# Loading V as rows of eight tokens and building its key spans on the chip

## The chip, the cores and the metric

The kernel runs on one core of one Trainium2 chip. The metric is the time of one execution in device microseconds. The program has the whole problem in one launch.

## The reference, cut to what matters

```python
q, k, v: (8, 8, 576, 64) float32            # batch, heads, tokens, head size
w_in: (512, 2048), w_out: (2048, 512)
scores = (q @ k.T) / 8, masked to 0 <= i - j < 64
attn   = softmax(scores) @ v
x      = attn as (8*576, 8*64)
h      = x @ w_in
out    = (h - tanh(h)) @ w_out               # (4608, 512)
```

A query sees itself and the 63 tokens before it. So a block of 64 queries needs 128 keys: its own block and the one before.

## The kernel before, in words

The work is in two kinds. **Attention** goes by pairs of heads: pair g is heads pr and pr + 4 of batch b, with g = 4b + pr, so there are 32 pairs. For each pair `load_qk` (L68) loads q and k on 72 partitions, each with 8 consecutive tokens of both heads (2 KB runs), on SP's queue. `cast` (L75) makes bf16 rows, mostly on GpSimd (POOL). `tr` (L150) transposes the rows on PE, 8 transposes each for q and for k, and moves the result out of PSUM: q's first head by ACT and its second by DVE, k by ACT. `scores` (L164) makes three groups of three 128x128 score tiles, keys on partitions, and ACT takes the exponential. `masking` (L172) multiplies by a mask on DVE. `pv` (L176) multiplies the three probability tiles of a group with V; a column of ones beside V gives the sums, DVE takes their reciprocal and scales the two heads. `x_tr` (L190) transposes the attention output of two pairs into the columns that the next stage reads. Tokens inside a block of 64 stand in a permuted order, which the mask and the output stores undo.

**V** stands in `vw`: for each block of 64 queries the lower 64 partitions hold the keys of the block before, the upper 64 those of the block itself, with 129 columns (two heads and the ones). `load_v` (L89) fills the upper half straight from HBM on POOL's software queue, which casts on the way, in runs of 64 numbers (256 bytes). `shift_v` (L95) copies the upper half to the lower half, one block further on, by an SBUF-to-SBUF DMA on SP.

**The two matrix products** go by chunks of 512 tokens, 9 chunks, 16 hidden tiles each. `hp_mm` (L208) is four matmuls of 512 columns and a tanh on ACT, `g_sub` (L217) the subtraction on DVE, `yp_mm` (L222) four matmuls of 512 columns of the output. `y_out` (L231) evicts an output block by ACT and stores it in two DMAs on SP. Weights are cast on the way by POOL's software queue, four parts of 512 KB each for `w_in` and for `w_out`.

The order is written out by hand. A counter h of half-steps runs in the loop at L281. Even half-steps issue a hidden group n = h/2, odd ones an output group that lies LAG = 24 hidden groups behind. `at(h, ...)` (L243) hangs the attention steps and loads on half-steps. For pair g they start at a = 3g - 21 in batch 0, 4g - 8 in batch 1 and 8g - 48 from batch 2 on, with the offsets of `TIGHT` and `WIDE`: in `WIDE` q's transposes at 0, k's at 1, scores at 4, 4, 6, the mask at 8, PV at 10, 13, 15. Each engine runs its instructions in this order, so a PE instruction whose data is late holds back all matmuls behind it. PSUM has two banks for the hidden groups, one for the output, two for transposes, two for scores and one for PV.

Of the kernel before, what the change touches and what calls it, by code (L numbers as in the profile page):

```python
# [15 lines left out]
def kernel(  # L16
# [13 lines left out]
    E, P = 8, S // 8  # L30
# [12 lines left out]
    qk_pool = ctx.enter_context(tc.tile_pool(name="qk", bufs=4))  # L43
# [31 lines left out]
    def cast(eng, g, n):  # L75
        t = row_pool.tile([P, E, 2, D], BF16, tag=n + "b", name=n + "b")
        o = t.rearrange("p e h d -> p h e d")
        i = stage.pop((g, n)).rearrange("p h (e d) -> p h e d", d=D)
        if eng is nc.scalar:
            nc.scalar.activation(o, i, ACT.Copy)  # L80
        else:
            eng.tensor_copy(o, i)  # L82
        rows[g, n] = t
# [26 lines left out]
    for g in range(NP):  # L110
        load_qk(g)
# [3 lines left out]
    for i in range(NV):  # L115
        nc.vector.memset(vw[i][0:64, :, 0, :], 0.0)
        nc.vector.memset(vw[i][64:128, :, :, 128], 1.0)
    load_v(0, 0, 1)
    for i in range(NR):
        nc.vector.memset(qT[i], 0.0)  # L120
        nc.vector.memset(kT[i][:, 0:64], 0.0)
    cast(nc.scalar, 0, "q")
    cast(nc.vector, 0, "k")
    load_v(0, 1, 2)
    nc.gpsimd.memset(mask, 1.0)

    nc.gpsimd.affine_select(mask, mask, compare_op=ALU.is_ge, fill=0.0,  # L127
                            base=-1, pattern=[[-1, 8], [-8, 8]], channel_multiplier=1)
    nc.gpsimd.affine_select(mask, mask, compare_op=ALU.is_ge, fill=0.0,
                            base=64, pattern=[[1, 8], [8, 8]], channel_multiplier=-1)  # L130
    cast_qk(1)
    load_v(0, 2, 3)
    cast_qk(2)
    load_v(0, 3, 4)
    load_w_in(0)
    cast_qk(3)
    for i in range(1, 4):
        load_w_in(i)
    for pr in range(NP):
        shift_v(0, pr, pr + 1)  # L140
# [9 lines left out]
    def tr(g, which):  # L150
        src = rows.pop((g, which)).rearrange("p e h d -> p e (h d)")
        tp = ps_tp.tile([128, E, P], BF16, tag="tp", name="tp")
        for e in range(E):
            nc.tensor.transpose(tp[:, e, :], src[:, e, :], ident[:P, :P])  # L154
        if which == "q":
            t = tp.rearrange("c e (j a) -> c j e a", a=8)
            o = qT[g % NR].rearrange("c j h (e a) -> c j h e a", e=E)
            nc.scalar.activation(o[0:64, :, 0], t[0:64], ACT.Copy)  # L158
            nc.vector.tensor_copy(o[64:128, :, 1], t[64:128])  # L159
# [4 lines left out]
    def scores(g, grp):  # L164
        sp = ps_s.tile([128, 3, 128], F32, tag="s", name="sp")
        for i in range(3):
            j = 3 * grp + i
            nc.tensor.matmul(sp[:, i, :], kT[g % NR][:, 64 * j:64 * j + 128],  # L168
                             qT[g % NR][:, j].rearrange("c h t -> c (h t)"), start=True, stop=True)
        nc.scalar.activation(PT[g % NR][:, 3 * grp:3 * grp + 3, :], sp, ACT.Exp, scale=scale)  # L170

    def masking(g):  # L172
        p = PT[g % NR].rearrange("p j (h t) -> p (j h) t", h=2)
        nc.vector.tensor_tensor(p, p, mask.unsqueeze(1).to_broadcast([128, 2 * NJ, 64]), ALU.mult)  # L174

# [13 lines left out]

    def x_tr(b, half, w0, w1):  # L190
# [134 lines left out]
```

## Time and profile before

| | |
|---|---|
| median of 3 runs | 398.25 us (393.59 to 398.42) |
| profiled execution | 396.17 us, span 392.9 us |
| PE busy | 329.2 us (84%) |
| DVE busy | 244.2 us (62%) |
| ACT busy | 184.8 us (47%) |
| POOL busy | 99.7 us (25%) |
| moved by DMA | 41.85 MB, 107 GB/s on the mean |

The span runs from the first to the last instruction; the time of the execution has a little around it. Busy shares are means over parts of the program with different limits, so the slices and the chain of waits tell more than the totals. A matmul's busy time overlaps with its neighbours'.

### The profile page before, as it was taken

To read this page: it belongs to the slowest core of one execution; us is meant where nothing else is said; L and a number is where in the kernel's file an instruction comes from. 1 tells how busy PE (TensorE), PEld (TensorE's weight loads), DVE (VectorE), ACT (ScalarE), POOL (GpSimd) and SP (SyncE) were. 2 spreads that over 40 slices of the span, in tenths; PEclk is the share of its full clock that TensorE was granted. 3 is DMA by queue.
4 is the path that set the end of the run, shared out by engine and by line. 5 is a ranking of instruction groups with operands and counts; after the bars stand their busy time and mean duration, and the time that the engine had idled before them with its cause. 6 is when DMAs were issued, how large, how long until landed. Compare 5 with 4: busy or idle time off the path is not lost.

```text
span 392.9 us, 6368 instructions
## 1 busy us (share of the span) xinstructions
PE 329.2 (84%) x2384; PEld 179.7 (46%) x2384; DVE 244.2 (62%) x553; ACT 184.8 (47%) x342; POOL 99.7 (25%) x107
## 2 busy tenths in 40 slices
PE   2124384883889999999999999999999999999884
PEld 2023242551455555555555555555554444444331
DVE  4116845676898888887887888878786433443000
ACT  4123134561466665656666656566653444444111
POOL 5941474400831342422243241330000000000000
PEclk9999999588899999999999999999999999999999
DMA  8999999998990968997599869761111010110221
GB/s 156 143 187 215 157 135 181 167 97 166 125 123 3 118 151 155 103 117 158 129 119 135 148 106 117 171 133 29 32 41 37 28 53 28 35 47 27 65 69 53
DMA packets 59006, 41.85 MB, mean 107 GB/s; under 512 B 39009, under 2 KB 43105, under 8 KB 58977
## 3 DMA queue, kind: packets, MB, share of 16 engines
q0 software_dynamic: 41536, 8.92, 61.0%
q1 hardware_dynamic: 17440, 32.54, 36.9%
q8 instruction: 18, 0.29, 0.4%
q14 instruction: 12, 0.09, 0.1%
HBM read 36.70 MB, written 9.44 MB: 117 GB/s over the span
## 4 chain that ended last, share of the span: by engine, by line
PE 72%; DMA 13%; DVE 4%; issue 3%; POOL 3%; ACT 3%; SPq 0%; POOLq 0%; ACTq 0%
PE yp L228 32%; PE hp L211 29%; DMA vw<-vw 6%; DMA w_in_sb<-in_moe_w_in_dram 5%; PE ov L181 4%; PE sp L168 3%; PE tp L154 3%; DMA kf<-in_k_dram 2%; DVE xs L187 1%; PE tpx L193 1%; POOL kb L82 1%; DVE gT L220 1%; ACT ysb L233 1%; POOL vw L91 1%; ACT th L214 1%
## 5 line engine op out<-in xcount | busy, mean ns | idle before, releaser
L211 PE MATMUL hp<-xT,w_in_sb 128*128 128x512 bf16 x576 | 152.9, 389 | 3.0 <-DVE gT L220 2.2
L228 PE MATMUL yp<-w_out_sb,gT 128*128 128x512 bf16 x576 | 145.0, 379 | 4.3 <-ACT ysb L233 4.3
L214 ACT ACTIVATE th<-hp 128x512 f32<-128x512 f32 x144 | 86.0, 597 | 131.9 <-PE hp L211 111.4
L220 DVE TENSOR_TENSOR gT<-hp,th 128x512 bf16<-128x512 f32 x144 | 99.5, 692 | 58.8 <-ACT th L214 56.7
L211 PEld LDWEIGHTS <-w_in_sb 128*128 128x128 bf16 x576 | 53.2, 100 | 52.6 <-issue 8.9
L228 PEld LDWEIGHTS <-gT 128*128 128x128 bf16 x576 | 52.4, 98 | 54.0 <-issue 5.9
L181 PE MATMUL ov<-vw,pt 128*128 128x129 bf16 x288 | 36.5, 240 | 41.7 <-DMA vw<-vw 12.9
L187 DVE TENSOR_TENSOR xs<-ov,rc 64x192 bf16<-64x192 f32 x192 | 68.1, 355 | 4.6
L170 ACT ACTIVATE pt<-sp 128x384 bf16<-128x384 f32 x96 | 43.3, 489 | 32.1 <-PE sp L168 31.9
L181 PEld LDWEIGHTS <-pt 128*128 128x128 bf16 x288 | 23.9, 104 | 65.5 <-issue 26.2
L82 POOL CAST qb<-qf 72x1024 bf16<-72x1024 f32 x31 | 34.7, 1121 | 74.2 <-DMA qf<-in_q_dram 49.5
L91 POOL DMA_DIRECT2D vw<-in_v_dram x28 | 25.7, 924 | 68.4 <-PE ov L181 55.0
L82 POOL CAST kb<-kf 72x1024 bf16<-72x1024 f32 x31 | 34.0, 1096 | 20.9 <-DMA kf<-in_k_dram 20.1
L184 DVE RECIPROCAL rc<-ov 128x3 f32<-128x3 f32 x96 | 17.1, 178 | 34.0 <-PE ov L181 31.3
L233 ACT ACTIVATE ysb<-yp 128x512 f32<-128x512 f32 x36 | 21.5, 597 | 28.2 <-PE yp L228 28.2
L168 PE MATMUL sp<-qt,kt 128*128 128x128 bf16 x288 | 30.2, 239 | 1.3 <-ACT kt L161 1.1
L174 DVE TENSOR_TENSOR pt<-pt,mask 128x1152 bf16<-128x1152 bf16 x32 | 30.3, 946 | 0.9
L168 PEld LDWEIGHTS <-kt 128*128 128x128 bf16 x288 | 23.1, 108 | 10.1 <-ACT kt L161 1.8
L161 ACT ACTIVATE kt<-tp 128x576 bf16<-128x576 bf16 x32 | 20.7, 648 | 7.3 <-PE tp L154 7.3
L159 DVE COPY qt<-tp 64x576 bf16<-64x576 bf16 x32 | 14.7, 460 | 13.1 <-ACT qt L158 12.8
L158 ACT ACTIVATE qt<-tp 64x576 bf16<-64x576 bf16 x32 | 20.2, 634 | 0.8 <-PE tp L154 0.8
L154 PE MATMUL tp<-ident,qb 72*128 72x72 bf16 x256 | 14.9, 208 | 5.7 <-POOL mask L127 5.7
(24 smaller groups left out, 96.4 us busy)
## 6 DMA issues: line engine op xcount, KB each, us to landing
qf<-in_q_dram SPq DMA_DIRECT2D x32, 288.0 KB
kf<-in_k_dram SPq DMA_DIRECT2D x32, 288.0 KB
out_dram<-ysb SPq DMA_DIRECT2D x72, 128.0 KB
vw<-in_v_dram POOLq DMA_DIRECT2D x12, 288.0 KB, 14.3
vw<-vw SPq DMA_DIRECT2D x6, 516.0 KB
w_in_sb<-in_moe_w_in_dram POOLq DMA_DIRECT2D x4, 512.0 KB, 15.5
w_out_sb<-in_moe_w_out_dram POOLq DMA_DIRECT2D x4, 512.0 KB, 27.2
vw<-in_v_dram POOLq DMA_DIRECT2D x16, 72.0 KB, 14.4
```

What stands on the lines that cost most here:

```text
L82: eng.tensor_copy(o, i)
L91: nc.gpsimd.dma_start(out=vw[b % NV][64:128, p0:p1, :, 64 * i:64 * i + 64].rearrange("p r j d -> p (r j) d"), in_=v[b, NP * i + p0:NP * i ...
L154: nc.tensor.transpose(tp[:, e, :], src[:, e, :], ident[:P, :P])
L168: nc.tensor.matmul(sp[:, i, :], kT[g % NR][:, 64 * j:64 * j + 128], qT[g % NR][:, j].rearrange("c h t -> c (h t)"), start=True, stop=True)
L170: nc.scalar.activation(PT[g % NR][:, 3 * grp:3 * grp + 3, :], sp, ACT.Exp, scale=scale)
L174: nc.vector.tensor_tensor(p, p, mask.unsqueeze(1).to_broadcast([128, 2 * NJ, 64]), ALU.mult)
L181: nc.tensor.matmul(ov[:, i, :], PT[g % NR][:, j, :], vw[b % NV][:, pr, j, :], start=True, stop=True)
L187: nc.vector.tensor_tensor(xs[b % 2][r, 3 * grp:3 * grp + 3, pr, :], ov[r, :, r], rc[r].to_broadcast([64, 3, 64]), ALU.mult)
L211: nc.tensor.matmul(hp, w_in_sb[:, ki, m * 128:(m + 1) * 128], chunk_tile(c)[:, ki, :], start=(ki == 0), stop=(ki == 3))
L214: nc.scalar.activation(th, hp, ACT.Tanh)
L220: nc.vector.tensor_tensor(gT[c][:, m, :], hp, th, ALU.subtract)
L228: nc.tensor.matmul(yps[c, s], gT[c][:, m, s * 128:(s + 1) * 128], w_out_sb[:, m, :], start=(m == 0), stop=(m == M - 1))
```

## The change

V is now loaded like q and k: 72 partitions with 8 consecutive tokens, two heads a load, 2 KB runs, in float32 on SP's queue. `cast_v` writes it as bf16 into `vb`, beside columns of ones. `keys_v` moves it to the upper half of `vw` by nine SBUF-to-SBUF DMAs on SP, one for each block of 64 tokens: 8 source partitions of 8 tokens become 64 partitions of 1040 bytes. `shift_v` fills the lower half by one DMA on SP as before, for batch 0 by two copies on DVE. q and k are loaded on 96 partitions with 6 tokens each, so a pair takes 6 transposes of 96 columns each for q and k. The order of tokens is then the natural one, and an output block is stored by one DMA.

Batch 0's attention, the loads of batches 1 and 2, their V and all the weights are written as one script, ahead of the loop. Batch 1's attention starts with half-step 0, four half-steps a pair, with both halves of q moved by ACT. From batch 2 on a pair still has eight half-steps, with other offsets, and V is loaded, cast, moved (32b - 53) and shifted (32b - 45) by half-steps. PSUM is one tile with its banks named by hand: two for the hidden groups, one for the output, one for transposes (in batches 0 and 1 k's are in the output's bank), one for scores, three for PV. A pair's normalising is one reciprocal and two multiplies, where it was three and six. LAG is 16.

```diff
-    E, P = 8, S // 8
+    E, P = 6, S // 6
+    EV, PV = 8, S // 8
...
-    qk_pool = ctx.enter_context(tc.tile_pool(name="qk", bufs=4))
+    qk_pool = ctx.enter_context(tc.tile_pool(name="qk", bufs=3))
+    v_pool = ctx.enter_context(tc.tile_pool(name="v", bufs=4))
...
-    g_pool = ctx.enter_context(tc.tile_pool(name="g", bufs=3))
+    g_pool = ctx.enter_context(tc.tile_pool(name="g", bufs=2))
+    psum = ctx.enter_context(tc.tile_pool(name="psum", bufs=1, space=PSUM))
+    ps = psum.tile([128, 8, 512], F32, name="ps")
...
+    vw = [const.tile([128, NJ, H, D + 1], BF16, name=f"vw{i}") for i in range(2)]
+    vb = const.tile([PV, EV, H, D + 1], BF16, name="vb")
...
-    def load_v(b, p0=0, p1=NP):
-        for i in range(2):
-            nc.gpsimd.dma_start(
-                out=vw[b % NV][64:128, p0:p1, :, 64 * i:64 * i + 64].rearrange("p r j d -> p (r j) d"),
-                in_=v[b, NP * i + p0:NP * i + p1].rearrange("h (j p) d -> p (h j) d", p=64))
+    def load_v(b, pr):
+        t = v_pool.tile([PV, 2, EV * D], F32, tag="vf", name="vf")
+        nc.sync.dma_start(out=t, in_=v[b, pr::NP].rearrange("h (p e) d -> p h (e d)", e=EV))
+        stage[b, pr, "v"] = t
+
+    def cast_v(b, pr, eng=nc.gpsimd):
+        move(eng, vb[:, :, 2 * pr:2 * pr + 2, 0:D].rearrange("p e h d -> p h e d"),
+             stage.pop((b, pr, "v")).rearrange("p h (e d) -> p h e d", d=D))
+
+    def keys_v(b):
+
+        for j in range(NJ):
+            nc.sync.dma_start(out=vw[b % 2][64:128, j].rearrange("p h c -> p (h c)"),
+                              in_=vb[8 * j:8 * j + 8].rearrange("p e h c -> p e (h c)"))
+
+    def shift_v(b, eng=None):
+        lo, hi = vw[b % 2][0:64, 1:NJ], vw[b % 2][64:128, 0:NJ - 1]
+        if eng is None:
+            nc.sync.dma_start(out=lo.rearrange("p j h c -> p (j h c)"), in_=hi.rearrange("p j h c -> p (j h c)"))
+        else:
+            eng.tensor_copy(lo[:, 0:4], hi[:, 0:4])
+            eng.tensor_copy(lo[:, 4:8], hi[:, 4:8])
...
+    def norm(g):
+        b, pr = divmod(g, NP)
+        ov = ps[:, 5:8, 0:390].rearrange("p n (i h c) -> p n i h c", h=2, c=D + 1)
+        rc = sm_pool.tile([128, 3, 3, 1], F32, tag="rc", name="rc")
+        nc.vector.reciprocal(rc, ov[:, :, :, 0, D:D + 1])
...
     def y_out(c, s):
         ysb = sm_pool.tile([128, d_model], F32, tag="ysb", name="ysb")
-        nc.scalar.activation(ysb, yps[c, s], ACT.Copy)
-        for u in range(2):
-            r0 = c * TOK + s * 128 + 64 * u
-            nc.sync.dma_start(out=out[r0:r0 + 64, :].rearrange("(a e) d -> e a d", e=E),
-                              in_=ysb[64 * u:64 * u + 64, :])
+        nc.scalar.activation(ysb, ps[:, 2, :], ACT.Copy)
+        r0 = c * TOK + s * 128
+        nc.sync.dma_start(out=out[r0:r0 + 128, :], in_=ysb)
```

The script (`play`) reads as follows, each step with its batch or pair: q loads q and k, v loads a pair of heads of V, c casts q and k, d casts V (p on POOL, a on ACT, d on DVE), k makes the nine moves, s the shift, m sets constants, w and o load parts of the weights, T transposes, S makes scores, M masks, V multiplies with V and normalises, X transposes the output.

```diff
+    at(-40, play, """
+        v00 v01 v02 v03 q0 d00p d01d d02d d03a q1 k0 c0ad T0 q2 c1pp m0 S0 q3 M0 T1
+        s0d S1 c2pp w0 M1 V0 T2 S2 V1 c3pp M2 T3 v10 v11 v12 v13 q4 V2 S3 X0 M3 V3 X1
+        d10p d11p d12p d13p q5 k1 w1 c4pp q6 c5pp s1 w2 q7 c6pp w3 q8 c7pp q9 v20 v21 c8pp o0 c9pp o1 v22 v23
+        d20p d21p o2 qa d22p d23p o3 qb k2 s2 
+    """)
+
+    for pr in range(NP):
+        g = NP + pr
+        a = 4 * pr
+        at(a, tr, g, "q", 3, nc.scalar)
+        at(a + 1, tr, g, "k", 2)
+        for i in range(3):
+            at(a + 3 + i, scores, g, i, 4)
+        at(a + 7, masking, g)
+        for i in range(3):
+            at(a + 10, pv, g, i)
+        at(a + 10, norm, g)
...
+    for g in range(2 * NP, B * NP):
         b, pr = divmod(g, NP)
...
+        a = 8 * g - 48
+        if b > 2:
+            at(a - 20, load_qk, g)
             at(a - 8, cast_qk, g)
...
+            at(32 * b - 78 + 6 * pr, load_v, b, pr)
+            at(32 * b - 73 + 6 * pr, cast_v, b, pr)
+        at(a, tr, g, "q", 3)
+        at(a + 2, tr, g, "k", 3)
+        for i in range(3):
+            at(a + 5 + 2 * i, scores, g, i, 4)
+        at(a + 11, masking, g)
+        for i in range(3):
+            at(a + 13 + i, pv, g, i)
+        at(a + 15, norm, g)
         if pr % 2 == 1:
...
+            at(a + 20, x_tr, b, pr // 2, 0, 4, 3)
+            at(a + 22, x_tr, b, pr // 2, 4, NJ, 3)
+    for b in range(3, B):
+        at(32 * b - 53, keys_v, b)
+        at(32 * b - 45, shift_v, b)
+
+    LAG = 16
```

## Rows read from the trace of the kernel before

**Rows 1.** The page: busy time by engine, and slices of the span.

```profile
PE 329.2 (84%) x2384; PEld 179.7 (46%) x2384; DVE 244.2 (62%) x553; ACT 184.8 (47%) x342; POOL 99.7 (25%) x107
...
PE   2124384883889999999999999999999999999884
...
DMA  8999999998990968997599869761111010110221
GB/s 156 143 187 215 157 135 181 167 97 166 125 123 3 118 151 155 103 117 158 129 119 135 148 106 117 171 133 29 32 41 37 28 53 28 35 47 27 65 69 53
```

**Rows 2.** The chain that ended last: start us, us, what.

```profile
50.30 16.33 DMA vw<-vw
...
86.61 8.60 DMA vw<-vw
...
118.62 0.87 PE yp L228 x4
...
360.95 0.88 PE yp L228 x4
...
362.50 3.63 PE yp L228 x16
...
387.84 0.60 ACT ysb L233
```

**Rows 3.** Windows: stretch, engines' busy us, PE clock, DMA share, GB/s.

```profile
16.00:22.00 6.00, 0.27 (x1) 0.14 (x2) 0.00 (x0) 0.00 (x0) 5.32 (x8) 1.00 3.67 74
28.00:30.00 2.00, 1.26 (x15) 1.09 (x14) 1.16 (x4) 1.85 (x4) 0.00 (x0) 1.00 1.15 270
94.00:102.00 8.00, 5.23 (x30) 2.95 (x30) 4.80 (x14) 1.47 (x3) 2.43 (x3) 0.57 0.80 185
96.00:98.00 2.00, 1.25 (x6) 0.73 (x7) 1.91 (x6) 0.00 (x0) 0.00 (x0) 0.50 0.81 196
102.00:110.00 8.00, 6.08 (x61) 3.58 (x58) 7.23 (x18) 4.94 (x10) 6.36 (x6) 1.00 4.24 86
```

**Rows 4.** Timeline of the front: start us, us, engine, line, operation, idle before.

```profile
0.81 0.43 SPq L72 DMA_DIRECT2D qf<-in_q_dram  x1
...
0.97 0.49 DVE L116 MEMSET vw<- 64x516 bf16 x1 [0.97 <-PEq L309]
...
4.54 1.06 ACT L80 ACTIVATE qb<-qf 72x1024 bf16<-72x1024 f32 x1 [2.46 <-DMA qf<-in_q_dram]
...
6.16 0.69 DVE L82 CAST kb<-kf 72x1024 bf16<-72x1024 f32 x1 [1.50 <-DMA kf<-in_k_dram]
...
9.61 1.04 POOL L82 CAST kb<-kf 72x1024 bf16<-72x1024 f32 x1 [0.76 <-DMA kf<-in_k_dram]
...
10.82 0.76 DVE L174 TENSOR_TENSOR pt<-pt,mask 128x1152 bf16<-128x1152 bf16 x1
...
51.10 3.16 PE L211 MATMUL hp<-xT,w_in_sb 128*128 128x512 bf16 x8
```

**Rows 5.** The weights' tile `w_in_sb`: landing times of its four loads.

```profile
DMA to landing us min/median/max: 11.1/15.5/22.7
```

**Rows 6.** Groups by line: busy us, mean ns, idle time before and its cause.

```profile
L187 DVE TENSOR_TENSOR xs<-ov,rc 64x192 bf16<-64x192 f32 x192 | 68.1, 355 | 4.6
L170 ACT ACTIVATE pt<-sp 128x384 bf16<-128x384 f32 x96 | 43.3, 489 | 32.1 <-PE sp L168 31.9
L184 DVE RECIPROCAL rc<-ov 128x3 f32<-128x3 f32 x96 | 17.1, 178 | 34.0 <-PE ov L181 31.3
L159 DVE COPY qt<-tp 64x576 bf16<-64x576 bf16 x32 | 14.7, 460 | 13.1 <-ACT qt L158 12.8
```

**Rows 7.** Timeline of ACT in the steady part.

```profile
126.85 0.60 ACT L214 ACTIVATE th<-hp 128x512 f32<-128x512 f32 x1 [0.44 <-PE hp L211]
127.34 0.63 ACT L158 ACTIVATE qt<-tp 64x576 bf16<-64x576 bf16 x1
128.24 0.65 ACT L161 ACTIVATE kt<-tp 128x576 bf16<-128x576 bf16 x1 [0.27 <-PE tp L154]
```

More of the change, by code (lines that the diff above doesn't have):

```diff
@@ L78, in cast @@
         i = stage.pop((g, n)).rearrange("p h (e d) -> p h e d", d=D)
[L79 to L82, printed above, removed]
+        move(eng, o, i)
         rows[g, n] = t
@@ L114, with more_constants @@
                             base=0, pattern=[[-1, 128]], channel_multiplier=1)
[L115 to L140, printed above, removed]
+    nc.vector.memset(qT[0], 0.0)
+    nc.vector.memset(kT[0][:, 0:64], 0.0)
+    nc.vector.memset(vb[:, :, :, D], 1.0)
+    def more_constants():
+        nc.vector.memset(qT[1], 0.0)
+        nc.vector.memset(kT[1][:, 0:64], 0.0)
+        for i in range(2):
+            nc.vector.memset(vw[i][0:64, 0], 0.0)
+        nc.gpsimd.memset(mask, 1.0)
+        nc.gpsimd.affine_select(mask, mask, compare_op=ALU.is_ge, fill=0.0,
+                                base=-1, pattern=[[-1, 64]], channel_multiplier=1)
+        nc.gpsimd.affine_select(mask, mask, compare_op=ALU.is_ge, fill=0.0,
+                                base=64, pattern=[[1, 64]], channel_multiplier=-1)
     xT = {}
@@ L147, in chunk_tile, with tr @@
         return xT[c]
-    def tr(g, which):
+    def tr(g, which, bank, eng=nc.vector):
         src = rows.pop((g, which)).rearrange("p e h d -> p e (h d)")
-        tp = ps_tp.tile([128, E, P], BF16, tag="tp", name="tp")
+        tp = ps[:, bank, :].bitcast(BF16)[:, 0:E * P].rearrange("c (e p) -> c e p", e=E)
         for e in range(E):
@@ L155, in tr @@
         if which == "q":
[L156 to L159, printed above, removed]
+            o = qT[g % NR].rearrange("c h (p e) -> c h p e", e=E)
+            t = tp.rearrange("c e p -> c p e")
+            nc.scalar.activation(o[0:64, 0], t[0:64], ACT.Copy)
+            move(eng, o[64:128, 1], t[64:128])
         else:
@@ L162, in tr, with scores @@
                                  tp.rearrange("c e p -> c p e"), ACT.Copy)
-    def scores(g, grp):
-        sp = ps_s.tile([128, 3, 128], F32, tag="s", name="sp")
+    def scores(g, grp, bank):
+        sp = ps[:, bank, 0:384].rearrange("p (i q) -> p i q", i=3)
         for i in range(3):
@@ L244, in at, with play @@
         items.setdefault(h, []).append(fn)
-    NG = B * NP
-    WIDE = dict(q=0, k=1, s0=4, s1=4, s2=6, mask=8, v0=10, v1=13, v2=15, x0=19, x1=22)
-    TIGHT = dict(q=0, k=1, s0=3, s1=3, s2=4, mask=5, v0=6, v1=7, v2=8, x0=10, x1=11)
-    at_v2 = {}
-    for g in range(NG):
+    ENG = dict(p=nc.gpsimd, a=nc.scalar, d=nc.vector)
+    def play(script):
+        for step in script.split():
+            what, n, more = step[0], int(step[1], 16), step[2:]
+            if what == "q":
+                load_qk(n)
+            elif what == "v":
+                load_v(n, int(more))
+            elif what == "c":
+                cast(ENG[more[0]], n, "q")
+                cast(ENG[more[1]], n, "k")
+            elif what == "d":
+                cast_v(n, int(more[0]), ENG[more[1]])
+            elif what == "k":
+                keys_v(n)
+            elif what == "s":
+                shift_v(n, ENG[more] if more else None)
+            elif what == "m":
+                more_constants()
+            elif what == "w":
+                load_w_in(n)
+            elif what == "o":
+                load_w_out(n)
+            elif what == "T":
+                tr(n, "q", 3, ENG[more or "d"])
+                tr(n, "k", 2)
+            elif what == "S":
+                for i, bank in enumerate((4, 0, 1)):
+                    scores(n, i, bank)
+            elif what == "M":
+                masking(n)
+            elif what == "V":
+                for i in range(3):
+                    pv(n, i)
+                norm(n)
+            elif what == "X":
+                x_tr(0, n, 0, 4, 3)
+                x_tr(0, n, 4, NJ, 2, nc.scalar)
@@ new lines @@
+    at(-40, play, """
[15 more added lines that the diff above has]
+        at(a + 10, norm, g)
+        if pr % 2 == 1:
+            at(a + 12, x_tr, 1, pr // 2, 0, 4, 3)
+            at(a + 13, x_tr, 1, pr // 2, 4, NJ, 2)
@@ L275 @@
-    for b in range(2, B):
-        a = at_v2[NP * (b - 1) - 1] + 1
-        at(a, load_v, b)
-        at(a + 22, shift_v, b)
-    LAG = 16 + 8
+            at(a + 20, x_tr, b, pr // 2, 0, 4, 3)
[4 more added lines that the diff above has]
+    LAG = 16
     for h in range(min(items), 2 * (16 * NC + LAG) + 2):
```

77 lines of the change are left out of this document (26 added, 51 removed).

## The prediction

> **What bounds the kernel now.** I read the page's slices first. PE is between 1 and 8 tenths busy in the first ten or eleven slices (to about 105 us), then full until slice 38, while the DMA engines are at nine tenths from the start to slice 17 [rows 1]. So the span has two parts. From the first output matmul at 118.62 us to 361.83 us PE is the bound: 119 hidden-layer groups and 120 output groups of four matmuls, 0.865 us each by the chain, are 206.7 us of these 243.2, and the other 36.5 us are the attention matmuls of about 21.5 head pairs, 1.70 us a pair [rows 2]. Idle time of DVE (62% busy) or ACT is worth nothing there.
>
> Before that, PE waits for V. The chain holds 16.33 and 8.60 us of the SBUF shift of V [rows 2], and it frees the PV matmuls of pair 8 only at 95.21 us; by the code that is half-step 26 (a = 16, plus 10). From there to 118.62 us PE did 10 hidden groups and about 3.1 pairs, 13.9 us of work in 23.4. [...]
>
> Why V is late shows in the fine windows: where the software queue loads V in 256-byte pieces, the DMA engines move 74 GB/s (16 to 22 us) or 86 (102 to 110 us); where q and k loads and weight loads run together, 270 [rows 3]. So a batch of V holds the engines some 8 us at the low rate.
>
> **The change, part by part.** The profiled execution took 396.17 us, span 392.9, so 3.3 us lie around it; the median of the runs is 2.1 us above it. I sum against the profiled one. Let t1 be the moment at which batch 2's shift lands and pair 8's PV can go. In the new schedule that is half-step 29 (a + 13), with 15 hidden groups done instead of 14.
>
> After t1: 129 hidden and 144 output groups, 273 x 0.865 = 236.1 us; attention of 23.2 pairs x 1.70 = 39.4. The transposes go from 16 of 72 columns to 12 of 96, the same 1152 columns a pair, and PV from 129 to 130 columns, so I leave 1.70. The tail: with LAG 16, four output blocks instead of six stand alone, each with a gap of 0.68 us for the eviction [rows 2], 2.7 us; after the last matmul 5.1 us (387.77 to 392.9). Two stores of 64 rows become one of 128; that may be worth -0.5 to +0.5 us, taken as 0. Sum 283.3 us. PE's gap before t1 will again bring the half clock; before, 8 us at 0.57 lost 3.4 us of full clock, so 3.5 us more. Together 286.8.
>
> How t1 comes about. V's first: four loads of 288 KB. In the old front the first load was consumed at 4.54 us, and the next consumers follow at 6.16 and (fourth load) 9.61 [rows 4]: 1.7 us a load. So the fourth V load lands at about 9.6 and its cast on ACT (1.06) ends at 10.7; the casts on POOL and DVE (1.04 and 0.69) hide under the loads. The nine moves are 585 KB. No row shows them; bounds are 2.2 us (270 GB/s) and 10 us (the shift's 516 KB in 8.60 us [rows 2]), and they stand behind the q and k loads of pairs 0 and 1, which land at 14 to 17. I take 20 for their end. The shift on DVE, two copies of 64x2080: the memset of 64x516 at 0.49 us gives 2.0 each [rows 4], the mask multiply (0.76 for 1152 columns, two inputs) 1.4 each; below, a quarter of that. I take 3 us together, on the path: 23. Three more pairs are then paced by POOL's casts (2.1 us a pair) and by each pair's own chain, about 3 us, so the first hidden group comes at 33 to 38 us, against 51.10 before. Its weights are issued at about 22 and take 11 to 15 us [rows 5], the same moment.
>
> From there bytes decide. Up to the shift of batch 2 the script moves 36 loads of 288 KB, three times 585 KB of moves, two shifts of 520 KB and eight weight loads of 512 KB: 17.7 MB. At the 270 GB/s of the best window that takes 65 us, at the 196 of 96 to 98 us, where only hardware loads ran, 90 [rows 3]. I take 230, since weight loads run beside them and the V stretches are gone: 77 us, and 1 us for the start, t1 = 78. (The old front had 15.3 MB behind it at 95 us, 160 GB/s by the mean of its slices [rows 1].) PE itself can't be there before about 69: with both halves of q on ACT a pair of batch 1 costs it 2 x 0.63 + 0.65 + 3 x 0.49 + two tanh of 0.60 = 4.6 us per four half-steps [rows 6, 7], so 29 half-steps from 36 end near 69.
>
> The sum: 78 + 286.8 = 364.8, plus 3.3 = **368 us**.
>
> Edits that I cost at nothing, and their cover. V's casts put 1.04 us a pair on POOL [rows 4], 20 of them in the steady part; V's 28 DMA issues leave it. POOL is 25% busy in all [rows 1]; without that slack its q and k casts would come late for the transposes, 8 half-steps later, by 1.04 us each. The nine moves a batch take SP about 9 x 0.43 = 3.9 us of issue [rows 4], and the shift makes SP wait until they land; behind it stand q and k loads (due 12 half-steps later) and stores (three buffers). One reciprocal and two multiplies instead of three and six save DVE near 1 us a pair by the fixed part of their 178 and 355 ns [rows 6]; PE is the bound, so it gains slack only. [...] The two gT buffers suffice with LAG 16, as the old chunk's last output group is issued before the new chunk's first write.
>
> Single banks for scores and for transposes: q's and k's transposes now share bank 3, two half-steps apart. From the end of q's transposes PE has two groups, 1.73 us, plus scores. ACT starts tanh and then q's copy 0.49 us after it and ends 1.1 us after tanh's start [rows 7]; DVE's half adds 0.46 [rows 6]. That is about 1.6 us: covered, by a few tenths. If it isn't, each pair loses those tenths.
>
> [...] The q, k loads moved about 288 KB per 1.7 us at 72 partitions, 170 GB/s [rows 4]. [...]
>
> **The rivals.** [...]
> (b) *Single banks stall PE.* 0.4 us for each of 24 pairs: 378 us. Against: DVE loses 1 us a pair of work.
> (c) *The front stays as slow as it was.* 17.7 MB at the old mean of 160 GB/s: t1 = 111, 401 us, no change. So too if the script's order (SP held at each shift until the moves land) makes the loading of three batches no quicker than before. Against it: the windows at 74 and 86 GB/s are V's alone.
> (d) *V misses its due time in every batch: slower.* In the steady part the moves are issued at 32b-53 and PV begins at 32b-35: 18 half-steps. Eight of them take 8 x 0.865 + 1.70 = 8.62 us, so 18 take 19.4. Moves and shift run one after the other. At 8.60 us per 516 KB they take 9.8 + 8.7 = 18.5, just in time; at 16.33 they take 35. At the middle, 27, PE waits 8 us in each of batches 3 to 7: 368 + 40 = 408 us. It begins to cost at 19.4 us, and makes the kernel slower by 2% from 27. For it: the shift that took 16.33 us; against: that one stood beside V's pieces, which go.
>
> **How the numbers follow.** Forecast 0.52, (a) 0.18, (b) 0.12, (c) 0.11, (d) 0.07. Two per cent, about what a measurement of this kernel can tell from no change, is 8 us: below 390.3 lie the forecast, (a) and (b), 0.82; (c) is within, 0.11; (d) is slower, 0.07. The range: below, t1 = 68 (PE's own pace) with no loss, 68 + 283.3 + 3.3 = 355; above, t1 = 101, 391, which takes in (a) and (b). 355 to 391 leaves (c) and (d) out, 0.18.
>
> **What would show it.** Right: no stretch of 6 us at 74 to 86 GB/s in the front; first hidden group at 33 to 38 us; first output group near 85, against 118.62; PE full from there; four lone output blocks. V's shift should still end the chain's last DMA wait, at 70 to 90 us. Wrong: a transfer of V, a weight load or POOL's casts still on the chain after 100 us; or gaps of PE in every pair in the steady part, ended by ACT's or DVE's copy of the transposes (b), or in every batch, ended by the shift (d). If the chain's last wait in the front isn't V but a q or k row's cast, the bytes were the wrong measure.

## The result, and the profile after

The changed kernel takes 379.12 us (median; 377.88 to 380.39), beside 395.92 us for the kernel before on the same chip: a ratio of 0.967, interval 0.958 to 0.976. It is faster, and 379 lies within the range, but the gain is 16.8 us by the medians and 12.9 by the ratio, where the forecast said some 30 (368 beside the 398.25 known then, 0.924). The medians given here are of all runs, the ratios leave out runs in a slower state of the chip: here two of the four of the kernel before (398.25 and 398.42 us), which leaves 392.06 for it, later two single runs of that kernel (399.80 and 400.94), one of v_soft (375.50) and one of v_soft_order (454.96). The page of the profiled execution (379.75 us, span 378.0), the lines that answer to [rows 1], with the granted clock:

```profile
PE 324.7 (86%) x2256; PEld 178.4 (47%) x2256; DVE 215.7 (57%) x354; ACT 190.4 (50%) x351; POOL 89.6 (24%) x108
...
PE   0554757625999999999999999999999999999985
...
PEclk9999999886999999999999999999999999999999
DMA  7699899978459637953984496465000010010111
GB/s 180 134 242 232 184 204 256 243 149 217 115 108 224 199 100 180 220 161 73 205 211 123 118 217 182 126 168 130 29 28 31 28 55 29 29 54 30 55 55 55
DMA packets 33485, 50.85 MB, mean 135 GB/s; under 512 B 2800, under 2 KB 23792, under 8 KB 33008
```

The change moves more than before, 50.85 MB against 41.85: V arrives as float32 where its loads had written bf16 (4.7 MB more), and is then moved once more on the chip (4.8). The page counts what a transfer writes, so a load that casts counts half of what it reads: a quarter of `w_in` is 1024 KB in float32 and stands there with 512.0 KB.

PE is full from slice 10 (counted from 0, 9.45 us each), two earlier than before, and has one hole, slices 8 and 9. The chain of waits shows what the hole is; it answers to [rows 2]:

```profile
78.11 6.76 DMA vw<-vb
...
84.95 4.48 DMA vw<-vw
89.47 0.38 PE ps L188 x2
...
93.89 0.86 PE ps L239 x4
...
120.08 0.97 PE ps L239 x4
...
356.00 0.88 PE ps L239 x4
...
357.55 3.63 PE ps L239 x16
...
374.20 0.60 ACT ysb L244
```

V's moves (`vw<-vb`) and then V's shift (`vw<-vw`) hold PE until 89.47 us. That is t1, forecast at 78. From it the span has 288.5 us left (forecast 286.8), and 1.75 us lie around the span (forecast 3.3): 89.5 + 288.5 + 1.75 = 379.75. So the miss is one term, t1, by 11.5 us. The windows up to it, with [rows 3]'s columns (last three: granted clock, DMA share, GB/s), the first 19 us once more in three parts:

```profile
0.00:20.00 20.00, 5.32 (x50) 4.61 (x51) 8.12 (x16) 8.07 (x13) 3.95 (x12) 1.00 0.71 163
20.00:40.00 20.00, 10.93 (x93) 8.76 (x91) 12.11 (x19) 6.53 (x14) 13.57 (x15) 1.00 1.01 226
40.00:55.00 15.00, 9.41 (x85) 5.38 (x84) 4.12 (x6) 11.30 (x21) 2.91 (x3) 1.00 0.99 194
55.00:79.00 24.00, 17.18 (x149) 10.12 (x147) 18.61 (x34) 13.45 (x25) 15.79 (x18) 0.93 1.12 243
79.00:85.00 6.00, 0.22 (x1) 0.10 (x2) 0.63 (x1) 0.00 (x0) 0.54 (x1) 0.78 0.51 119
85.00:89.50 4.50, 0.03 (x1) 0.03 (x1) 0.00 (x0) 0.00 (x0) 0.00 (x0) 0.50 0.69 159
...
0.00:2.50 2.50, 0.00 (x0) 0.00 (x0) 0.69 (x3) 1.28 (x1) 0.69 (x6) 1.00 0.21 33
2.50:10.70 8.20, 0.00 (x0) 0.00 (x0) 1.39 (x2) 1.09 (x2) 1.04 (x1) 1.00 0.96 226
10.70:19.00 8.30, 5.04 (x47) 4.39 (x48) 5.10 (x9) 5.54 (x11) 2.21 (x5) 1.00 0.58 126
```

Rate times length, summed, is 17.95 MB: the bytes were counted right (17.7), and at 230 GB/s they would take 78.0 us. Row by row, time over what the row's bytes need at 230: +5.8 us in the first 20, +0.3, +2.3, -1.4, and +4.3 in the last 10.5. The rate failed at the start and at the end, around V's moves and shift. Of the 5.8 us at the start 2.1 pass before the loads are under way; V's loads and the first q and k loads then run at 226 GB/s, no loss; and 3.8 are lost from 10.7 to 19 us, while batch 0's nine moves hold SP's queue.

The timeline of SP, POOL, PE, ACT and DVE, rows that the steps below use:

```profile
10.69 0.84 ACT L75 ACTIVATE qb<-qf 96x768 bf16<-96x768 f32 x1
...
11.86 0.56 DVE L77 CAST kb<-kf 96x768 bf16<-96x768 f32 x1 [3.27 <-DMA kf<-in_k_dram]
...
13.04 0.82 POOL L77 CAST qb<-qf 96x768 bf16<-96x768 f32 x1 [7.28 <-DMA qf<-in_q_dram]
...
17.36 0.70 DVE L117 COPY vw<-vw 64x2080 bf16<-64x2080 bf16 x1
19.02 0.70 DVE L118 COPY vw<-vw 64x2080 bf16<-64x2080 bf16 x1 [0.96 <-DMA vw<-vb]
...
33.36 6.87 SPq L109 DMA_DIRECT2D vw<-vb  x9
...
38.75 0.63 PE L223 MATMUL ps<-xT,w_in_sb 128*128 128x512 bf16 x1
...
46.08 0.55 SPq L115 DMA_DIRECT2D vw<-vw  x1
...
71.03 1.07 POOL L77 CAST vb<-vf 72x1024 bf16<-72x1024 f32 x1 [0.75 <-DMA vf<-in_v_dram]
...
72.12 7.65 SPq L109 DMA_DIRECT2D vw<-vb  x9
...
84.95 0.53 SPq L115 DMA_DIRECT2D vw<-vw  x1
...
89.47 0.38 PE L188 MATMUL ps<-vw,pt 128*128 128x130 bf16 x2 [10.10 <-DMA vw<-vw]
```

The last cast of batch 2's V ends at 72.1; from there to t1 it is 17.4 us: 7.65 to issue nine moves, 5.1 until the last has landed, 4.5 for the shift. PE itself is ready at 79.37 and stands still for 10.10 us.

The rate of the moves is best seen in the DMA slices of 70 to 90 us, 0.5 us each (share in tenths, then GB/s):

```profile
DMA  9999999899999998998656555543100099849279
GB/s 249 246 250 252 248 246 207 200 222 194 213 215 220 229 252 165 179 173 169 120 124 120 124 128 137 149 131 131 67 31 0 0 266 266 183 100 250 82 287 260
```

As long as q, k and weight loads run beside the moves the engines are at 8 or 9 tenths, at 165 to 252 GB/s. From 79.5 us only the moves and the rest of one weight load (issued at 72.04, such a load takes 12 us) are in flight, and the share drops to 5 or 6 tenths at 120 to 149 GB/s.

### The profile page after: what moved, and what is told of

Same layout as the page of the kernel before. It is cut to its first block, busy times and chain, and to the rows that moved or that the text cites. A ratio compares the mean times of both kernels' runs of the same rounds, so it can differ in the third digit from the quotient of the medians.

```text
span 378.0 us, 6022 instructions
## 1 busy us (share of the span) xinstructions
PE 324.7 (86%) x2256; PEld 178.4 (47%) x2256; DVE 215.7 (57%) x354; ACT 190.4 (50%) x351; POOL 89.6 (24%) x108
## 2 busy tenths in 40 slices
DMA packets 33485, 50.85 MB, mean 135 GB/s; under 512 B 2800, under 2 KB 23792, under 8 KB 33008
## 4 chain that ended last, share of the span: by engine, by line
PE 75%; DMA 3%; DVE 1%; ACT 1%; issue 0%; ACTq 0%; SPq 0%
PE ps L239 34%; PE ps L223 30%; PE ps L188 4%; PE ps L176 3%; PE ps L162 3%; DMA vw<-vb 2%; PE ps L205 2%; DMA vw<-vw 1%; ACT ysb L244 1%; DVE gT L232 1%; DVE xs L199 0%; DVE qt L77 0%; ACT qt L166 0%; DVE xT L77 0%; DVE rc L195 0%
## 5 line engine op out<-in xcount | busy, mean ns | idle before, releaser
L223 PE MATMUL ps<-xT,w_in_sb 128*128 128x512 bf16 x576 | 150.8, 384 | 2.4 <-DVE gT L232 2.2
L232 DVE TENSOR_TENSOR gT<-ps,th 128x512 bf16<-128x512 f32 x144 | 99.4, 690 | 86.2 <-ACT th L226 85.0
L239 PE MATMUL ps<-w_out_sb,gT 128*128 128x512 bf16 x576 | 145.8, 379 | 3.0 <-ACT ysb L244 3.0
L226 ACT ACTIVATE th<-ps 128x512 f32<-128x512 f32 x144 | 86.1, 598 | 83.6 <-PE ps L223 78.0
L178 ACT ACTIVATE pt<-ps 128x384 bf16<-128x384 f32 x96 | 46.2, 490 | 59.8 <-PE ps L176 59.7
L77 POOL CAST vb<-vf 72x1024 bf16<-72x1024 f32 x29 | 30.9, 1064 | 122.9 <-DMA vf<-in_v_dram 91.4
L199 DVE TENSOR_TENSOR xs<-ps,rc 64x576 bf16<-64x576 f32 x64 | 48.3, 755 | 1.5
L188 PE MATMUL ps<-vw,pt 128*128 128x130 bf16 x288 | 32.7, 237 | 16.6 <-DMA vw<-vw 11.2
L176 PE MATMUL ps<-qt,kt 128*128 128x128 bf16 x288 | 32.9, 233 | 5.7 <-ACT kt L169 3.3
L162 PE MATMUL ps<-ident,qb 96*128 96x96 bf16 x192 | 14.7, 217 | 16.6 <-ACT qb L75 11.6
L77 POOL CAST kb<-kf 96x768 bf16<-96x768 f32 x31 | 27.0, 870 | 6.1 <-DMA kf<-in_k_dram 4.8
## 6 DMA issues: line engine op xcount, KB each, us to landing
w_in_sb<-in_moe_w_in_dram POOLq DMA_DIRECT2D x4, 512.0 KB, 11.0
w_out_sb<-in_moe_w_out_dram POOLq DMA_DIRECT2D x4, 512.0 KB, 12.0
```

The source lines that it names most:

```text
L178: nc.scalar.activation(PT[g % NPT][:, 3 * grp:3 * grp + 3, :], sp, ACT.Exp, scale=scale)
L188: nc.tensor.matmul(ps[:, 5 + grp, 130 * i:130 * i + 130], PT[g % NPT][:, j, :], vw[b % 2][:, j, 2 * pr:2 * pr + 2, :], start=True, stop=True)
L199: nc.vector.tensor_tensor(xo[r, :, :, pr, :], ov[r, :, :, h, 0:D], rc[r].to_broadcast([64, 3, 3, 64]), ALU.mult)
L223: nc.tensor.matmul(hp, w_in_sb[:, ki, m * 128:(m + 1) * 128], chunk_tile(c)[:, ki, :], start=(ki == 0), stop=(ki == 3))
L226: nc.scalar.activation(th, hp, ACT.Tanh)
L232: nc.vector.tensor_tensor(gT[c][:, m, :], hp, th, ALU.subtract)
```

## The experiments

All were run with the kernel before beside them, at 393 to 401 us; ratios are to it. "After" below is the changed kernel, 379.12 us, 0.967. It was not run again beside them, and its ratio stands on a lower time of the kernel before (392.06 us, in the others 395.6 to 396.7), so differences to it below are of medians from two sessions. How far its front varies by itself two runs show that leave the front as it is: PV of pair 8 goes at 87.07 us in lag15 and 88.22 in lag24, where after's own trace has 89.47.

**1. The shift off SP's queue.** `s2_dve`:

```diff
-        d20p d21p o2 qa d22p d23p o3 qb k2 s2
+        d20p d21p o2 qa d22p d23p o3 qb k2
+    at(28, shift_v, 2, nc.vector)
```

> Batch 2's shift is made by two copies on DVE at half-step 28 instead of one DMA. Theory A (after the last V cast the moves and the shift run as a chain of latencies, with the DMA engines half idle): the copies cost 2 x 0.70 us against 4.48 us of the shift, so pair 8's PV starts near 86.4 instead of 89.5 us and the kernel is 3 us shorter, 376 us. Theory B (the bytes set the moment, whatever their order): 0.53 MB less at 230 GB/s, 2.3 us, but only if the engines were full; with the engines at 159 GB/s in that stretch it gives the same 3. Rival C (PE would have lost the time anyway, on weights or on DVE): 0.

372.74 us, 0.942 (0.936 to 0.948). PV of pair 8 goes at 81.89 instead of 89.47, 7.6 us earlier, and the time falls by 6.4, twice what was expected. What t1 gains comes out of the total nearly one for one, and the shift as a DMA was on the path for all of its time. The rest has two sources: the moves are issued 1.4 us sooner (70.69), which is within the spread above, and the copy is in two halves, of which PE needs only the first. That one starts at 81.14 us, when its moves are in; the second waits for the last moves until 83.74. The DMA had to wait for all nine.

**2. Two pairs' loads behind the moves.** `qk_late`:

```diff
-        d20p d21p o2 qa d22p d23p o3 qb k2 s2
+        d20p d21p o2 d22p d23p o3 k2 s2 qa qb
```

> The loads of pairs 10 and 11 stand behind batch 2's moves and shift on SP instead of ahead of them; nothing else changes. Theory A: the moves no longer wait behind 1.18 MB in the queue; they land about 5 us earlier, the shift too, PV of pair 8 near 84 us, time 374 to 375 us. Rival: the moves are slow by themselves (half of the engines), so that they land at most 1 us earlier: 378 to 379 us. If the casts of pairs 10 and 11 then come late, transposes of pair 10 wait after 95 us and part of the gain goes back.

374.12 us, 0.948 (0.943 to 0.952). PV at 85.15. The moves are issued at 70.70, landed by 80.53 and the shift takes 4.46 us more: 9.8 us for nine moves with fewer loads around them, the upper end (10) of the bounds in the prediction. Of the 4.3 us at PV 1.4 lie ahead of the moves' issue, as in s2_dve; the loads beside the moves cost some 3 us (9.9 us from the first issue to the shift's, 12.8 in after). What is left the moves need by themselves. In its last stretch before the shift no other transfer is left; the window (columns of [rows 3]) and the only data queue then active:

```profile
78.20:80.50 2.30, 0.00 (x0) 0.00 (x0) 0.00 (x0) 0.00 (x0) 0.00 (x0) 0.51 0.43 116
```

```profile
q1 hardware_dynamic: 292, 0.27, 43.0%
```

The moves, each from 8 source partitions, keep the engines busy there by a share of 0.43, at 116 GB/s.

**3. Both.** `both`, k2 ahead of qa and qb, and the shift on DVE:

> Both edits: loads of pairs 10 and 11 behind the moves, and batch 2's shift on DVE. Theory A: the two gains add, PV of pair 8 near 81 us, close to PE's own arrival at 79 us: 371 us. If PE's own pace were the limit behind it, less: no earlier than 79 us, 369 us at best.

370.68 us, 0.938 (0.932 to 0.945); PV at 80.51, PE waiting 3.31 for the copy. The two gains overlap, since both shorten the same chain.

**4. How many partitions a load uses: q and k back on 72.** `rows72`:

```diff
-    E, P = 6, S // 6
+    E, P = 8, S // 8
```

> q and k on 72 partitions (8 tokens, 2 KB runs, 8 transposes of 72 columns) with everything else of the changed kernel kept. If 96 partitions gave q and k a third more engines, the first q and k loads land 1.6 us apart instead of 1.2, and the 24 loads of the front lengthen it by 4 to 9 us: 383 to 388 us. If the engines are shared out so that the number a transfer uses does not matter in the front: 378 to 380 us.

386.83 us, 0.980 (0.973 to 0.988): 7.7 us slower than after. Its timeline (ACT, DVE, POOL) of the first q and k loads, each released by its landing, against the three rows of after above:

```profile
9.82 1.06 ACT L75 ACTIVATE qb<-qf 72x1024 bf16<-72x1024 f32 x1 [0.28 <-DMA qf<-in_q_dram]
...
11.20 0.69 DVE L77 CAST kb<-kf 72x1024 bf16<-72x1024 f32 x1 [3.44 <-DMA kf<-in_k_dram]
...
12.59 1.04 POOL L77 CAST qb<-qf 72x1024 bf16<-72x1024 f32 x1 [7.19 <-DMA qf<-in_q_dram]
```

In these rows loads of 288 KB are 1.38 us apart with 72 partitions (212 to 214 GB/s) and 1.18 with 96 (250). But they don't come sooner with 96: the third is there at 12.59 us with 72 and at 13.04 with 96. V's four loads ahead of them, on 72 partitions in both kernels, come 1.35 to 1.39 us apart here and about 1.6 in after; no run shows why. The first hidden group isn't later either (37.78 against 38.75). The loss comes after that: in the windows of 20, 15 and 24 us from 20 us on the engines move 213, 175 and 234 GB/s (after 226, 194, 243), and PV of pair 8 goes at 93.37, 3.9 us later. So the edit is worth 7.7 us by the medians (4.9 between the two profiled executions), for which the prediction's sum had no term. How many engines one load uses no run shows, and how much of the loss is the partitions' alone neither: a cast on POOL takes 1.04 us where it took 0.82, and the runs are of 2 KB instead of 1.5.

**5. The same for V: rows of four tokens.** `v4rows`: 512 tokens as 128 partitions of four, the last 64 tokens as 16 partitions of their own; a move reads 16 source partitions, where after reads 8, and V's loads have runs of 1 KB, where after has 2.

```diff
-    EV, PV = 8, S // 8
+    EV, PV = 4, 128
+    PT4 = (S - EV * PV) // EV
...
-                              in_=vb[8 * j:8 * j + 8].rearrange("p e h c -> p e (h c)"))
+                              in_=(vb[16 * j:16 * j + 16] if j < 8 else vt).rearrange("p e h c -> p e (h c)"))
```

> V in rows of four tokens: 512 tokens on 128 partitions and the last 64 of all heads on 16, so that each move has 16 source partitions in place of 8; the loads have 1 KB runs. Only the moves matter at the end of the front. If a move with 8 source partitions uses half of the DMA engines, the busy share of the engines while only moves run (0.43 to 0.60 in the changed kernel) goes to near 1, the last moves land 2 to 4 us sooner and the time is 375 to 377 us. If the moves are held by SP's issue (0.6 us each) or by the size of their runs, the share and the time stay: 378 to 380 us, or more with the smaller runs of the loads.

370.30 us, 0.932 (0.926 to 0.939), better than both theories said. Two rows of SP, its chain, then its DMA slices of 60 to 80 us:

```profile
27.99 5.18 SPq L121 DMA_DIRECT2D vw<-vb  x8
...
36.91 0.52 SPq L127 DMA_DIRECT2D vw<-vw  x1
```

```profile
68.82 5.50 DMA vw<-vb
74.38 4.33 DMA vw<-vw
...
78.75 0.38 PE ps L201 x2
```

```profile
DMA  9999999999999999999999997310000999584999
GB/s 255 269 268 267 270 259 269 268 270 255 252 221 235 252 241 252 235 235 239 243 220 238 231 233 170 74 44 19 0 0 0 266 266 250 116 166 121 363 336 102
```

The gain is nearly all ahead of the moves. Batch 2's are issued from 62.13 us on (72.12 in after; 69.86 and 71.08 in lag15 and lag24, so some 2 us are spread). The first 20 us move 207 GB/s where after moved 163, the 15 us from 40 on 239 where it moved 194. SP's rows place the 10 us: 5.4 are there when batch 1's moves go out (27.99 against 33.36), as V's loads land sooner (batch 0's last is cast from 7.60 us on, 9.52 in after); 3.8 more come between those moves and batch 1's shift (8.9 us against 12.7), a time in which SP's queue loads little else. Loads and moves both took part, and partitions and runs changed together. From the first issue to PV it is 16.6 us, against 17.35: issue, landing and shift in series gain 0.7 us by the wider moves. The share does stay at nine tenths until the data ends at about 72.5 us (moves and the last weight load, 220 to 238 GB/s from 70 us on), where after's fell to 5; but then 1.5 us pass at 46 GB/s until the shift goes out, and the shift carries nothing in its first us.

What the partitions do by themselves isn't shown. Moves with 8 source partitions have a share of 0.43 in qk_late. For q and k 72 partitions against 96 are 1.38 against 1.18 us, 17%; but V's loads, on 72 partitions in both kernels, differ as much (1.36 against 1.6). No run here shows the moves of 16 partitions alone.

**6. V's loads earlier.** `v2_first`: batch 2's V loads ahead of q8, q9 and w_out, k2 ahead of qa and qb, pair 6's load ahead of k1, both shifts on DVE, V in rows of eight:

```diff
+        d10p d11p d12p d13p q5 q6 k1 w1 c4pp c5pp w2 q7 c6pp w3 v20 v21 v22 v23 q8 c7pp q9
+        d20p d21p d22p d23p k2 c8pp o0 c9pp o1 o2 o3 qa qb
```

> The script reordered: batch 2's V is loaded ahead of pairs 8 and 9 and of all of w_out, its moves stand ahead of the loads of pairs 10 and 11, q and k of pair 6 ahead of batch 1's moves, and both shifts of batches 1 and 2 are copies on DVE (half-steps 9 and 28). Theory A (the moment at which batch 2's V is ready sets the end, and it is a matter of order): V is ready at about 70 us, before PE arrives; then batch 1's own pace on PE, ACT and DVE decides (PV of pair 8 at 74 to 77 us), and the time is 364 to 367 us. Theory B (the bytes decide, in whatever order): the late w_out or pairs 8 and 9 now hold PE back as long as V did, and the time stays at 370 to 372 us, as with both smaller edits.

367.96 us, 0.926 (0.918 to 0.935), a little short. V is no longer late for batch 2: PV goes at 78.14, after 0.49 us of waiting for DVE's copy, which stands behind the mask (the profile names a q load there, that of pair 10, which lands in the same moment). But pair 8's q now is: its cast on POOL comes behind V's, and PE waits 3.32 us for it at 61.77. And batch 3's shift, 9.18 us long, makes PE wait 1.08 us at 113.75. Loads that go ahead push others back.

**7. The best of 5 and 6.** `v4_order`: rows of four; q6 ahead of k1, qa and qb last, both shifts on DVE:

```diff
-        d10p d11p d12p d13p q5 k1 w1 c4pp q6 c5pp s1 w2 q7 c6pp w3 q8 c7pp q9 v20 v21 c8pp o0 c9pp o1 v22 v23
-        d20p d21p o2 qa d22p d23p o3 qb k2 s2
+        d10p d11p d12p d13p q5 q6 k1 w1 c4pp c5pp w2 q7 c6pp w3 q8 c7pp q9 v20 v21 c8pp o0 c9pp o1 v22 v23
+        d20p d21p o2 d22p d23p k2 o3 qa qb
+    at(9, shift_v, 1, nc.vector)
+    at(28, shift_v, 2, nc.vector)
```

> V in rows of four tokens (16 source partitions a move), and the order mended: q and k of pair 6 ahead of batch 1's moves, the loads of pairs 10 and 11 behind batch 2's moves, both shifts on DVE. Theory A (engines of the moves and order both set when V is ready, and PE's own pace in batch 1 is next): PV of pair 8 goes at 71 to 74 us, the time is 361 to 364 us. Rival (PE, ACT and DVE of batch 1 are the limit already with four-token rows alone, where PE arrived at 71 us and waited until 78.75): 366 us or more.

**363.37 us, 0.917 (0.911 to 0.922), faster than both kernels.** Its timeline of PE: first hidden group, PV of pair 8 (its first three matmuls), first output group.

```profile
35.03 1.44 PE L236 MATMUL ps<-xT,w_in_sb 128*128 128x512 bf16 x3 [0.69 <-ACT xT L78]
...
72.09 0.23 PE L201 MATMUL ps<-vw,pt 128*128 128x130 bf16 x1 [0.79 <-DVE pt L195]
73.48 0.27 PE L201 MATMUL ps<-vw,pt 128*128 128x130 bf16 x2 [1.16 <-DVE vw L129]
...
77.70 1.23 PE L252 MATMUL ps<-w_out_sb,gT 128*128 128x512 bf16 x4
```

PE waits 1.16 us for V, not 10.10. The hole is gone; from the first hidden group to PV it now takes 38.5 us, and the waits that are left are short.

**8. V's path alone undone.** `v_soft`: POOL's software queue loads V in pieces of 64 numbers, cast on the way, straight to key spans, as in the kernel before; no rows, no moves. The shift and all else are as in after, but for one thing: from batch 3 on V's loads are issued at 32b - 68 + 2pr instead of 32b - 78 + 6pr. The diff, cut:

```diff
-        nc.sync.dma_start(out=t, in_=v[b, pr::NP].rearrange("h (p e) d -> p h (e d)", e=EV))
+        for i in range(2):
+            nc.gpsimd.dma_start(out=vw[b % 2][64:128, :, 2 * pr + i, 0:D],
+                                in_=v[b, NP * i + pr].rearrange("(j p) d -> p j d", p=64))
```

> V's path alone undone: POOL's software queue loads V with the cast straight into the upper half of the key spans, in runs of 64 numbers; no float32 rows, casts or moves. Script, q and k on 96 partitions, PSUM and LAG as in the changed kernel; the shifts stay. If V's new path is what shortened the front, each of three batches holds the engines some 8 us at 74 to 86 GB/s again, PV of pair 8 goes 8 to 15 us later than at 89.5 us and the time is 388 to 395 us. If the new path only changed one late V for another (its moves end 13 us after the last cast), 377 to 381 us.

371.48 us, 0.936 (0.930 to 0.942): the theory behind the 388 to 395 falls, and the rival's 377 to 381 does too. Without the part that gives the change its name the kernel is 7.6 us *faster*. Its windows:

```profile
20.00:40.00 20.00, 8.95 (x86) 8.02 (x85) 11.79 (x19) 5.66 (x12) 10.45 (x13) 1.00 2.56 158
...
55.00:79.00 24.00, 16.15 (x153) 9.82 (x155) 19.12 (x34) 15.00 (x29) 14.78 (x20) 1.00 1.79 165
```

The DMA issues of its last window, and PV of pair 8:

```profile
vw<-in_v_dram POOLq DMA_DIRECT2D x12, 72.0 KB, 13.7
...
81.13 0.38 PE L185 MATMUL ps<-vw,pt 128*128 128x130 bf16 x2 [2.51 <-DMA vw<-vw]
```

The low rates of [rows 3] are back (158 and 165 GB/s where after has 226 and 243) and the first hidden group is later (43.17 us against 38.75). Part of that rate is only the count: a piece load of one head stands there with 72 KB, what it writes, and reads twice that. Still V is ready sooner: the pieces land where the shift reads them and the shift goes out at 70.61, when after is still at its last cast (to 72.1) and has 12.9 us of moves before it. The shift takes longer beside the pieces (10.48 us against 4.48), and PV goes at 81.13, 8.3 us before after's. A slow transfer in one hop beat a quick one in three (load, cast, moves). Up to there it also writes some 3.6 MB less, three batches of V and of moves; no run separates hops from bytes further than these rows do.

**9. And with the order mended.** `v_soft_order`: v_soft with the script of 7 and both shifts on DVE.

> V by the software queue, cast on the way, as in v_soft (371.48 us), with the order of v4_order (363.37 us): pair 6's loads ahead of k1, those of pairs 10 and 11 last, the shifts of batches 1 and 2 on DVE. In v_soft the shift of batch 2 was issued at 70.61 us and took 10.48, and pair 8's PV began at 81.13. Theory A: the on-chip moves buy nothing once the order is mended, the two ways of bringing V are worth the same: DVE's copies end near 73, PV of pair 8 at 73 to 76, 363 to 366 us, level with v4_order. Theory B: the rows of V are the better way once their order is right, since 256-byte pieces hold up the q and k loads: PV of pair 8 at 78 or later, 368 us or more.

374.28 us, 0.941 (0.932 to 0.950): no gain over v_soft (0.936, 0.930 to 0.942), the intervals overlap. Its timeline of PE:

```profile
44.30 0.63 PE L220 MATMUL ps<-xT,w_in_sb 128*128 128x512 bf16 x1
...
82.28 0.23 PE L185 MATMUL ps<-vw,pt 128*128 128x130 bf16 x1 [1.16 <-DVE pt L179]
83.01 0.38 PE L185 MATMUL ps<-vw,pt 128*128 128x130 bf16 x2 [0.49 <-DVE vw L113]
```

The number is theory B's; the place isn't quite. Batch 2's V isn't what PE waits for (its copy comes 0.49 us late, behind the mask). From the first hidden group to the wait's end it takes 38.7 us (83.01 - 44.30), in v4_order 38.5 (73.48 - 35.03). All of the difference lies ahead: the first hidden group at 44.30 against 35.03, 9.3 us, of 9.4 between the two profiled executions (373.30 and 363.90). Batch 0's copies begin at 26.48 us here, behind the pieces, and at 15.17 there. So the rows of V do pay, but in the first batch, and only where their shape and order keep the later ones off the path.

**10. What LAG is worth.** `before_lag16` (the kernel before, LAG from 24 to 16) and `lag24` (after, with 24 and three gT buffers):

```diff
-    LAG = 16
+    LAG = 16 + 8
```

> The kernel before with LAG 16 instead of 24, nothing else. The tail has four output blocks alone instead of six, 2 x 0.68 us less of gaps, and output groups fill PE from half-step 33 on, where the old front leaves gaps (some 9 us between 95 and 118 us are lost). By the tail alone: 1.4 us less, 394.5 us. If the output groups fill the gaps too: up to 6 us less, 390 us. If they only push back the hidden groups: no change.

> The changed kernel with LAG 24 and three gT buffers, as the kernel before had. The kernel before gained 5.4 us by LAG 16. If LAG's gain is the tail (2 x 0.68 us) and work for PE in the gaps of the front, here, where no gap is left behind half-step 33, only the tail remains: 380 to 381 us. If it is a gain of its own size: 384 us.

before_lag16: 391.32 us beside 396.69, 0.985 (0.978 to 0.993), 5.4 us gained. lag24: 385.15 us, 0.972 (0.967 to 0.977), 6.0 us lost against after's median. The shorter tail is only a part: two output blocks more alone, at a gap of 0.68, make 1.4. In lag24 the first output group comes at 107.50 us against 93.89, and until then the odd half-steps hold no group. PE waits there for DVE's masks and copies (0.3 to 1.2 us each between 94 and 104 us); that the shorter half-steps are the reason is argued, not shown.

**11. The pace.** `lag15`, LAG one less, so that output groups fall elsewhere in the pattern of single banks:

> LAG 15 instead of 16 in the changed kernel. With 16 the eviction of an output block falls on the half-step of q's transposes and right behind the exponential of a score group on ACT, and the next output group takes 0.97 us on the chain instead of 0.86, 24 times: 2.6 us. If that coincidence is the cause, the step goes away or moves, and with a quarter block less in the tail the time is 376 to 377 us. If the 0.11 us belong to the transposes themselves (two matmuls' switch on PE), nothing changes: 379 us.

377.70 us, 0.952 (0.944 to 0.960), 1.4 us under after, between the two values expected. The front, which the edit leaves alone, is 2.4 us sooner here (PV of pair 8 at 87.07), of 2.7 between the profiled executions, so the 1.4 aren't LAG's. In after two pairs take 17.58 us; here 17.60. The output group of 0.97 us after q's transposes becomes 0.86, and a wait turns up in another place. The coincidence isn't what sets the pace.

## Why the prediction came out as it did

**The step that failed** is "From there bytes decide ... I take 230": t1 as 17.7 MB over one rate. Bytes were right (17.95 MB), the rate was 201 GB/s on the mean. It failed where V's moves and shift run one after the other with little beside them: 126 GB/s at a share of 0.58 around batch 0's moves (3.8 us lost), 119 and 159 GB/s from batch 2's last moves to PV (4.3 us); 2.1 us more went before the first loads were under way, for which 1 was taken. The prediction's own times for batch 0 (585 KB between 10.7 and 20 us) had such a stretch in them; the sum by bytes didn't.

Rival (a), V's own transfers slow, named the number: t1 = 91 and 381 us, measured 89.5 and 379.1. That is in part luck: no run shows the rates that its 91 us were worked out from. What the runs show in their place: while V's loads run the engines do 226 GB/s, beside the 230 taken. The moves are slow, 116 GB/s at a share of 0.43 where nothing else is in flight (qk_late), but why isn't shown: with 16 source partitions the way from issue to PV is 16.6 us instead of 17.35. Still more partitions for V, with shorter runs, pay, by 8.8 us in v4rows, through loads that land sooner and a shorter time at batch 1's moves. I gave (a) 0.18; from 79 us on, at shares of 0.51 and 0.69, there was too little else in flight to fill the engines.

**At the end bytes were the wrong measure.** Between V's last cast and PV stood 17.4 us of serial work: nine issues, landing, shift. Order and a copy in place of the shift, 0.53 MB less in all, gave 8.4 us (both). I had put moves and shift in series in rival (d), for the steady part, and left them out of t1; in the steady part that rival didn't show.

**"A batch of V holds the engines some 8 us at the low rate"**, and its removal as the source of the gain: not borne out for the change as written. v_soft has the low rate and is 7.6 us faster. The pieces slow the front, but V's three hops cost more than they. And the 74 to 86 GB/s were set beside 270 as if they counted the same thing: a casting load is counted by what it writes, half of what it reads (72 KB of 144 for a piece load of one head).

**LAG and the partitions.** LAG I had priced at a tail of 2.7 us, the 96 partitions, in the sum, at nothing. Measured: 5.4 to 6.0 us for LAG, 7.7 us for 96 partitions. With -12.9 to -16.8 in all, and V's path at +7.6, the rest (three batches in one script, banks, one norm a pair) would be about -7 to -11 if these added up; it wasn't run alone.

**Right, or nearly:** the first hidden group at 38.75 us (33 to 38 said). Batch 0's V: moves landed by 19.0 us (20 said); the two DVE copies took 1.4 us, 0.70 each (3 taken for both; a copy at a quarter of 1.4 us, the lower bound, no run shows). The sum after t1, 288.5 against 286.8, with errors that offset: two pairs take 17.58 us instead of 2 x 8.62 = 17.24, 3.9 us follow the last matmul's end (374.13), not 5.1, and the half clock after t1 costs some 1.5 us (0.72 on the mean from 89.5 to 95), not 3.5. The tail: 356.88 to 357.55 is one of four gaps, 0.67 us. Not right: the first output group came at 93.89 us, not near 85, as t1 was late. Rival (b) is there and small: 21 output groups of the chain take 0.97 us instead of 0.86, 2.3 us where 9.6 were said; lag15 moves that step elsewhere without a quicker pace. Rival (c) is out: PE was full from 90 us on.

**The floor** I had put at 69 us (33 us from the first hidden group). v4_order shows 38.5 us, 73.5, and v_soft_order, with another way for V, 38.7.

## What to carry to other kernels

A transfer's worth isn't its bytes over the best rate: the front's ran at 201 GB/s on the mean where 230 was taken, and at 116 where the moves were alone, so look at what else is in flight. Where the partitions of loads were changed, run lengths with them, more partitions were the quicker (7.7 us for q and k, 8.8 for V). A detour over on-chip moves cost 7.6 us here while 17.4 us of it lay in the open; count issue, landing and shift in series from the last cast to the first reader, and put loads that nobody needs yet behind it. When a change has several parts, undo its headline part alone: here, as first written, it cost time, and the parts beside it had earned the gain; with rows of four and a mended order it paid.

## What was not expected of the hardware

The issue of a small SBUF-to-SBUF move (65 KB) takes SP 0.60 us at the least, 0.62 at the median, and nine take 7.65 us in batch 2 and 6.4 to 6.7 from batch 4 on; a q load took 0.43 [rows 4], the value that the prediction used. A DVE copy of 64x2080 bf16 took 0.70 us, less than the mask multiply of 128x1152 (0.75 at the median); in v4_order the later ones took 1.30 to 1.36 us; no run shows why. And PE's hole is paid twice: the granted clock falls to 0.50 within it, and when PE is back a hidden group takes 1.71 us at 90.16, at 92.77 again 0.86 (the page's clock slices 8 and 9 show 8 and 6 tenths; the 8 in slice 7 lies ahead of the hole), as in [rows 3].
